# P*V of two key units in one burst, four work banks in one pool, seven P tiles

## The chip, the cores and the metric

The kernel runs on one core of one Trainium2 chip. The metric is the device time of one execution in microseconds (us). The profile is one execution, taken by the hardware profiler; its times count from the first instruction of the span.

## The reference

One layer gates between two branches that read the same x of 2048 rows and 512 columns. All tensors are bf16.

```python
g = sigmoid((x * gate_w).sum(-1, keepdims=True))
out = g * A(x) + (1 - g) * B(x)

# B: gated GELU, inner width 1792
B = (gelu(x @ w_gate) * (x @ w_up)) @ w_down

# A: 32 heads of 16, four segments of 512 rows; causal inside a segment, a memory across segments
for s in range(4):
    p     = softmax(qs @ ks.T / 4 + causal_mask)
    a_dot = p @ vs
    a_mem = (phi(qs) @ M) / (phi(qs) @ z + 1e-6)      # phi(t) = t + 1 if t > 0 else exp(t)
    o     = sigmoid(beta) * a_mem + (1 - sigmoid(beta)) * a_dot
    M += phi(ks).T @ vs;  z += phi(ks).sum(rows)
A = concat(o) @ wo
```

## The kernel before

Everything stays on chip between the loads of x and the weights and the stores of the result. The work is cut into the four segments of 512 rows. Per segment there are projections of Q, K and V, the memory terms, the attention, and the three products of the gated GELU. The last product and the output projection accumulate into the same PSUM bank, in groups of 18 full matmuls (14 of `w_down`, 4 of `wo`). The other full groups have four matmuls of 512 columns, and then ScalarE or VectorE empties the bank (lines 441, 438, 847, 868).

**Attention.** The 32 heads are taken in four units of eight heads (`t`) per segment, 16 units in all. Four heads of a unit share one instruction group: one half `j = 0`, the other half `j = 1`; these halves are the two "key units" (they use `kpad_0` and `kpad_1`). The logits are computed transposed, keys on partitions, by matmuls on four row tiles of 32 (line 737) into the four banks `X` (one tensor, `psXALL`). The causal triangle packs into five fills per unit, in the order A0, B0, C, A1, B1; C holds a block of each half. Each fill is followed by one exp on ScalarE over 128x2048 elements into a P tile (`PT`, line 745), and by one or two masks on GpSimd for the diagonal blocks (line 757). P*V of one half (function `pv`, line 770) is a burst of 16 matmuls on four column tiles, four key blocks by four heads, with 512, 384, 256 and 128 columns. It needs A, B and C of its half. The values carry a column of ones, so that the sum of the softmax comes out as column 17. VectorE then transposes the bank into `Tb` (line 778), and `norm` (lines 781 to 800) divides, scales and adds the result to the memory's part.

**PSUM.** Eight banks: four are `X`, one is `Pb` for P*V alone (`psP`), and three are a pool `psW0` to `psW2` for all other groups. A group (`Grp`) takes a bank of the pool at its first matmul and gives it back after the instruction that empties it.

**P tiles.** Six, taken in turn; P*V of half 0 frees A0 and B0 before A1 and B1 are filled, in the order of the program's text.

**The order of the work.** A planner (`Sched.schedule`) simulates the five engines with estimated durations. It picks, over all engines, the ready task that can start first, and among equals the one with the highest priority: the longest path to the end plus an entry of the table `BIAS` for its name. The result is one fixed order per engine; semaphores then guard what depends on what. Full groups are issued in pieces of two matmuls, so that logits steps can come between. A task of P*V (`tiled == "pv"`) has rules of its own (lines 191 to 195): when it is ready and the last thing on TensorE was a logits step, it goes at once; otherwise its start counts as 3 us later (`PATIENCE`), except for the very last half of a segment.

Of the kernel before, what the change touches and what calls it, by code (L numbers as in the profile page):

```python
# [11 lines left out]
F32 = mybir.dt.float32  # L12
# [8 lines left out]
P = 128  # L21
ATT_SCALE = 0.25
EPS = 1e-6
R_PT = 6
N_W = 3
PSUM_KEYS = ("X", "P", "W")
DMA_RATE = 330.0e3
PATIENCE = 3.0
OPEN_BONUS = 6.0
BIAS = {  # L30
    "D0": 18, "D1": -562, "D2": 14, "D3": -73, "G0": -139, "G1": 25, "G2": -43, "G3": 47, "GdT0": -152,
    "GdT1": 3, "GdT2": -4, "Gev0": 175, "K0": -203, "K1": 238, "K2": -374, "K3": -9, "Q1": 3, "Q2": 76, "U0":
    171, "U1": 59, "U3": 121, "Um1": 326, "Um2": 354, "Um3": 115, "V0": 4, "V2": 186, "Vev0": 4, "Vev1": -6,
    "Vev3": 31, "den1": 56, "den2": -1, "den3": -5, "denp2": -17, "denp3": -33, "exp0": 78, "exp1": 166,
    "exp2": -1, "exp3": -154, "exsT0": 2, "exsT1": 2, "exsT2": 2, "exsT3": -9, "fin0": 4, "fin1": 14, "fin3":
    -350, "gate0": 9, "gate1": -152, "gelu0": 224, "gelu1": 4, "gelu2": 15, "gelu3": -19, "gexs0": -69,
    "gexs1": -410, "gexs2": 50, "gts0": 4, "gts1": 2, "gts2": 84, "gts3": 40, "kp0": -1283, "kp1": -135,
    "kp2": 26, "kp3": -7, "msk1": 189, "msk2": -33, "msk3": 3, "mz0": 100, "mz2": -453, "mzacc0": -243,
    "mzacc1": 341, "mzacc2": -115, "mzbd0": 25, "mzbd1": -47, "mzbd2": 70, "norm0": 47, "norm1": 44, "norm2":
    -15, "norm3": 382, "num1": 15, "num2": 4, "num3": 54, "nump1": -275, "nump2": -19, "nump3": 84, "oTd1":  # L40
    187, "oTd2": -109, "omg": -23, "pkT0": -16, "pkT1": -268, "pkT2": 70, "pkc0": 270, "pkc1": -17, "pkc2":
    -442, "pke0": -30, "pke1": -21, "pke2": 380, "pqc1": -30, "pqc2": -20, "pqc3": -25, "pqe1": 5, "pqe2": -6,
    "pqe3": 79, "pv0": -19, "pv1": 2, "pv2": 64, "pv3": 95, "pvt0": 1, "pvt1": -237, "pvt2": -42, "pvt3": -2,
    "qk0": 224, "x1": 389, "x3": 21
}
HOP = {PE: 0.17, ACT: 0.07, DVE: 0.07, POOL: 0.10, SP: 0.0}

# [66 lines left out]
class Sched:  # L114
# [32 lines left out]
    def schedule(self):  # L147
# [35 lines left out]
        while len(order) < n:  # L183
            best = None
            due = min([ready_at[t.id] for t in ready[ACT] if t.tiled == "exp"] + [1e9])
            for e in ENGINES:
                for t in ready[e]:
                    st = max(cur[e], ready_at[t.id])
                    if e == ACT and t.tiled != "exp" and st + t.est[e] > due + 0.1:
                        continue  # L190
                    if t.tiled == "pv":
                        if last_pe == "qk" and ready_at[t.id] <= cur[e]:
                            best = ((-1.0, 0.0, t.id), e, t)
                            continue
                        st += t.patience
                    if t.grp is not None and t.grp.bank is None:
                        if not bank_free:
                            continue
                        st = max(st, min(bank_free.values()))
                    open_ = t.grp is not None and t.grp.bank is not None  # L200
                    k = (st, -t.prio - (OPEN_BONUS if open_ else 0.0), t.id)
                    if best is None or k < best[0]:
                        best = (k, e, t)
            assert best is not None, "deadlock in task graph"
            (st, _, _), e, t = best
            if t.tiled == "pv":
                st = max(cur[e], ready_at[t.id])
            if e == PE:
                last_pe = t.tiled
            for a in t.alts:  # L210
                ready[a].discard(t)
            t.eng = e
            t.start = st
            t.finish = st + t.est[e]
            cur[e] = t.finish
            avail = t.finish
            if t.nbytes:
                dma_free = max(t.finish + 2.2, dma_free) + t.nbytes / DMA_RATE
                avail = dma_free
            g = t.grp  # L220
            if g is not None:
                if g.bank is None:
                    g.bank = min(bank_free, key=lambda b: bank_free[b])
                    del bank_free[g.bank]
                g.left -= 1
                if g.left == 0:
                    bank_free[g.bank] = t.finish + HOP[e]
            order.append(t)
            for s in t.succs:
                npred[s.id] -= 1  # L230
                hop = 0.0 if (e == PE and s.alts.keys() == {PE}) else HOP[e]
                ready_at[s.id] = max(ready_at[s.id], avail + hop)
                if npred[s.id] == 0:
                    for a in s.alts:
                        ready[a].add(s)
# [103 lines left out]
def dve_t(n, mode=1, psum=False, ap=False):  # L339
    return max(0.19, 0.155 + n / mode / 960.0 + (0.06 if ap else 0.0))  # L340
# [11 lines left out]
def _build(es, nc, A_x, A_wq, A_wk, A_wv, A_wo, A_beta, B_w_gate, B_w_up, B_w_down, gate_w, out):  # L352
    def sb(name, shape, dtype=BF):
        return es.enter_context(nc.sbuf_tensor(name, shape, dtype))
# [9 lines left out]
    Vaug = [sb(f"vaug{i}", [P, 4, 32, 17]) for i in range(2)]  # L364
    otok = sb("otok", [P, 4, 512])
    oT = [sb(f"oT{i}", [P, 4, 512]) for i in range(2)]
    Tb = [sb(f"tb{i}", [P, 2, 512], F32) for i in range(2)]
    obf = [sb(f"obf{i}", [P, 512]) for i in range(2)]
    ott = [sb(f"ott{i}", [P, 512]) for i in range(2)]
    hT = [sb(f"hT{i}", [P, NFT, 512]) for i in range(2)]  # L370
# [30 lines left out]

    XALL = es.enter_context(nc.psum_tensor("psXALL", [P, 2048], F32))
    X = [XALL[:, g * 512:(g + 1) * 512] for g in range(4)]
    Pb = es.enter_context(nc.psum_tensor("psP", [P, 512], F32))
    banks = []
    for i in range(N_W):
        w = es.enter_context(nc.psum_tensor(f"psW{i}", [P, 512], F32))
# [12 lines left out]
    def task(name, eng, instrs, **kw):  # L420
        return S.add(Task(name, {eng: instrs}, **kw))
# [69 lines left out]
    for c0, c1 in ((0, 128), (128, 512)):  # L491
        for key, w, src in (("wk", wk, A_wk), ("wq", wq, A_wq)):
# [9 lines left out]
    wdma("wd", SP, wd[:], r4(B_w_down), 1835008)  # L502
    wdma("wo", SP, wo[:], r4(A_wo), 524288)

    task("warmP", PE, [Instr(lambda e: e.matmul(Pb[:, :], warm[:, 0:128], warm, start=True, stop=True), [wkey],
                             [("P",)], 0.43)], bias=5001.0)
    for i in range(8):
        gw = Grp(banks)
        task(f"warm{i}", PE, [Instr(lambda e, gw=gw: e.matmul(gw.f32()[:, :], warm[:, 0:128], warm, start=True,  # L509
                                                              stop=True), [wkey], [gw.key], 0.43)],  # L510
             grp=gw, bias=5000.0 - i)
# [213 lines left out]
    def attention(s):  # L725
        sl = s % 2
        for t in range(4):
# [32 lines left out]
                task(f"msk{s}_{t}{name}", POOL, minstrs)  # L760
                return slot

            def pv(j, sa, sbk, sc):
                i2 = t % 2
                instrs = []
                for kb in range(4):
                    slot, c0 = ((sa, 0), (sbk, 0), (sc, 256 * j), (sbk, 384))[kb]
                    for q in range(4):
                        h = 8 * t + 2 * q + j
                        instrs.append(Instr(lambda e, q=q, kb=kb, slot=slot, c0=c0, h=h: e.matmul(  # L770
                            Pb[32 * q:32 * q + 17, 128 * kb:512], Vaug[sl][:, kb, h, :],
                            PT[slot][:, q, c0:c0 + 512 - 128 * kb], start=(kb == 0), stop=(kb == 3),
                            tile_position=(0, 32 * q)),
                            [("PT", slot), ("Vaug", sl, kb)], [("P",)], 0.043))
                p = task(f"pv{s}_{t}_{j}", PE, instrs)
                p.tiled = "pv"
                p.patience = 0.0 if (t, j) == (3, 1) else PATIENCE
                task(f"pvt{s}_{t}_{j}", DVE, [Instr(lambda e: e.transpose(Tb[i2][:, j, :], Pb[:, :]),  # L778
                                                    [("P",)], [("Tb", i2, j)], dve_t(512))])

            def norm():
                i2 = t % 2
                tv = Tb[i2][:].rearrange("p j (b c) -> p j b c", c=32)
                ov = bass.AP(obf[i2], 0, [[512, P], [16, 2], [32, 16], [1, 16]])
                rb = sc1[i2][:].rearrange("p j (b o) -> p j b o", o=1).to_broadcast([P, 2, 16, 16])
                gd = GdT[sl][:, 2 * t:2 * t + 2, :]
                ok = [("oT", sl, qt, t) for qt in range(4)]
                dst, dk = (oT[sl][:, t, :], ok) if s == 0 else (ott[i2][:], [("ott", i2)])
                ins = [
                    Instr(lambda e: e.reciprocal(recip[i2][:], tv[:, :, :, 16]), [("Tb", i2, 0), ("Tb", i2, 1)],  # L790
                          [("recip", i2)], 0.35),
                    Instr(lambda e: e.tensor_tensor(sc1[i2][:], recip[i2][:], gd, ALU.mult),
                          [("recip", i2), ("GdT", sl)], [("sc1", i2)], 0.34),
                    Instr(lambda e: e.tensor_tensor(ov, tv[:, :, :, 0:16], rb, ALU.mult),  # L794
                          [("Tb", i2, 0), ("Tb", i2, 1), ("sc1", i2)], [("obf", i2)], 0.79),
                    Instr(lambda e: e.transpose(dst, obf[i2][:]), [("obf", i2)], dk, dve_t(512))]  # L796
                if s > 0:
                    ins.append(Instr(lambda e, t=t: e.tensor_tensor(oT[sl][:, t, :], oT[sl][:, t, :], ott[i2][:],  # L798
# [3 lines left out]
            a0 = fill("A0", [(0, 0, 512, 0)], [0])  # L802
            b0 = fill("B0", [(0, 1, 384, 0), (0, 3, 128, 384)], [0, 384])
            cc = fill("C", [(0, 2, 256, 0), (1, 2, 256, 256)], [(0, 256)])
            pv(0, a0, b0, cc)
            a1 = fill("A1", [(1, 0, 512, 0)], [0])
            b1 = fill("B1", [(1, 1, 384, 0), (1, 3, 128, 384)], [0, 384])
            pv(1, a1, b1, cc)
            norm()

    gelu_of = {}
# [197 lines left out]
```

## Time and profile before

| | us |
|---|---|
| median of three executions | 281.25 |
| lowest and highest | 280.67 and 281.27 |
| the profiled execution | 280.67 |
| its span, first to last instruction | 279.0 |
| TensorE busy | 267.8 (96%) |
| ScalarE busy | 215.4 (77%), of it 150.1 in 80 exps of 1876 ns |
| VectorE busy | 192.1 (69%) |
| GpSimd busy | 103.8 (37%), of it 83.8 in masks |
| P*V bursts on TensorE, line 770 | 23.1, 512 matmuls |
| transposes of P*V, line 778 | 22.8, 32 of 713 ns |

In the profile PE is TensorE's matmuls, PEld its weight loads, ACT is ScalarE, DVE VectorE, POOL GpSimd and SP the queue that issues DMAs. Busy time of a matmul includes a modelled end that overlaps the next one, so a row of n matmuls of 512 columns is longer than n steps. A few matmul records are missing from a trace; the loads then show one more than the matmuls. In the chain of work each piece has its start, its length and its line; a piece begins where the one that released it ended.

### The profile page before, as it was taken

The page shows a single profiled execution, that of the slowest core. Times are in us where ns is not written, and L with a number is a line of the kernel's source. Part 1 is how long each engine was busy: PE and PEld are TensorE (multiplying, and loading weights), DVE is VectorE, ACT ScalarE, POOL GpSimd, SP SyncE. Part 2 cuts the span into 40 slices and gives each one's busy share as a digit, 9 for nine tenths or more (in the row PEclk, how much of TensorE's full clock was granted, in tenths as well). Part 3 has the DMA queues.
Part 4 walks back from the last instruction along what each step waited for, and adds up shares of the span by engine and source line. Part 5 has one row for each costly group of instructions (what it writes and reads, how often), then busy time and mean ns, then how long its engine had stood idle before and what let it go on. Part 6 is the DMA issues. An engine that isn't in the chain of part 4 may idle for free.

```text
span 279.0 us, 5322 instructions
## 1 busy us (share of the span) xinstructions
PE 267.8 (96%) x2148; PEld 113.4 (41%) x2186; DVE 192.1 (69%) x334; ACT 215.4 (77%) x168; POOL 103.8 (37%) x197
## 2 busy tenths in 40 slices
PE   8999999999999999999999999899999999999995
PEld 3443334344444434543443343334344335443342
DVE  1587999979786997899509897667542657584442
ACT  3788988789989967788779887767878676687622
POOL 8156438531004245734102348434400334333410
PEclk9999999999999999999999999999999999999999
DMA  6999930000022331011000300100000000130002
GB/s 194 200 382 359 206 59 2 0 4 0 0 58 57 40 75 59 19 40 38 2 0 19 59 0 2 36 22 2 21 0 0 0 4 2 37 77 22 18 2 75
DMA packets 29697, 15.30 MB, mean 55 GB/s; under 512 B 21224, under 2 KB 29672, under 8 KB 29672
## 3 DMA queue, kind: packets, MB, share of 16 engines
q1 hardware_dynamic: 29672, 14.96, 22.6%
q8 instruction: 17, 0.28, 0.4%
q14 instruction: 8, 0.07, 0.1%
HBM read 8.14 MB, written 2.10 MB: 37 GB/s over the span
## 4 chain that ended last, share of the span: by engine, by line
PE 87%; DVE 5%; ACT 4%; issue 2%; POOL 1%; ACTq 0%; DVEq 0%
PE psW L424 68%; PE psXALL L737 9%; PE psP L770 6%; ACT pt L745 4%; DVE kpad_1 L624 2%; PE psXALL L424 1%; PE psW L509 1%; DVE hT L868 1%; POOL pt L757 1%; DVE hT L441 0%; DVE oT L798 0%; DVE otok L684 0%; DVE obf L794 0%; PE psXALL L514 0%; DVE ott L796 0%
## 5 line engine op out<-in xcount | busy, mean ns | idle before, releaser
L745 ACT ACTIVATE pt<-psXALL 128x2048 bf16<-128x2048 f32 x80 | 150.1, 1876 | 41.1 <-PE psXALL L737 27.1
L757 POOL TENSOR_SCALAR_AFFINE_SELECT pt<-pt 128x512 bf16<-128x512 bf16 (+1 forms) x112 | 83.8, 750 | 159.5 <-ACT pt L745 150.7
L868 DVE TENSOR_TENSOR hT<-psW,hT 128x512 bf16<-128x512 f32 x56 | 37.1, 685 | 26.7 <-PE psW L424 26.5
L424 PE MATMUL psW<-xT,wu 128*128 128x512 bf16 x217 | 51.4, 380 | 1.4 <-issue 0.6
L424 PE MATMUL psW<-xT,wg 128*128 128x512 bf16 x215 | 50.6, 380 | 1.3 <-issue 0.8
L424 PE MATMUL psW<-wd,hT 128*128 128x512 bf16 x201 | 50.1, 380 | 1.0 <-issue 0.8
L778 DVE STREAM_TRANSPOSE tb<-psP 128x512 f32<-128x512 f32 x32 | 22.8, 713 | 22.5 <-PE psP L770 22.4
L424 PEld LDWEIGHTS psW<-xT,wu 128*128 128x128 bf16 x224 | 20.3, 97 | 27.8 <-DVE hT L868 2.9
L424 PEld LDWEIGHTS psW<-xT,wg 128*128 128x128 bf16 x224 | 20.4, 98 | 26.2 <-issue 2.1
L424 PEld LDWEIGHTS psW<-wd,hT 128*128 128x128 bf16 x210 | 18.6, 98 | 22.4 <-issue 4.0
L770 PE MATMUL psP<-pt,vaug 128*17 128x256 bf16 (+3 forms) x512 | 23.1, 300 | 0.0
L847 ACT ACTIVATE hT<-psW 128x512 bf16<-128x512 f32 x28 | 16.3, 597 | 6.1 <-PE psW L424 6.1
L424 PE MATMUL psW<-xT,wk 128*128 128x512 bf16 x60 | 15.9, 379 | 0.7 <-issue 0.3
L737 PE MATMUL psXALL<-qT,kpad_0 32*128 32x512 bf16 (+3 forms) x256 | 15.8, 301 | 0.4 <-ACT exs L641 0.2
L737 PE MATMUL psXALL<-qT,kpad_1 32*128 32x512 bf16 (+3 forms) x256 | 15.8, 301 | 0.3 <-ACT pt L745 0.3
L424 PE MATMUL psW<-xT,wq 128*128 128x512 bf16 x61 | 15.3, 379 | 0.5 <-DVE mzacc L710 0.2
L424 PE MATMUL psW<-wo,oT 128*128 128x512 bf16 x56 | 14.6, 380 | 0.9 <-DVE ost L896 0.7
L424 PE MATMUL psW<-wv,xT 128*128 128x512 bf16 x62 | 15.3, 380 | 0.1
L441 DVE CAST hT<-psW 128x512 bf16<-128x512 f32 x21 | 14.0, 680 | 1.8 <-PE psW L424 1.6
L770 PEld LDWEIGHTS psP<-pt,vaug 128*17 128x17 bf16 x512 | 10.0, 89 | 12.9 <-issue 5.3
L652 POOL COPY exsT<-exs 32x4 f32<-32x4 f32 x64 | 13.5, 212 | 3.6
L836 ACT ACTIVATE hT<-hT 128x2048 bf16<-128x2048 bf16 (+2 forms) x6 | 12.7, 2184 | 0.0
(92 smaller groups left out, 241.0 us busy)
## 6 DMA issues: line engine op xcount, KB each, us to landing
out_dram<-ost SPq DMA_DIRECT2D x16, 128.0 KB, 1.7
wg<-in_B_w_gate_dram SPq DMA_DIRECT2D x2, 896.0 KB, 6.0
wu<-in_B_w_up_dram SPq DMA_DIRECT2D x2, 896.0 KB, 10.5
wd<-in_B_w_down_dram SPq DMA_DIRECT2D x1, 1792.0 KB, 16.6
hT<-in_A_x_dram SPq DMA_DIRECT2D x2, 256.0 KB, 2.9
wv<-in_A_wv_dram SPq DMA_DIRECT2D x1, 512.0 KB, 5.9
wo<-in_A_wo_dram SPq DMA_DIRECT2D x1, 512.0 KB, 12.9
wq<-in_A_wq_dram SPq DMA_DIRECT2D x1, 384.0 KB, 5.0
```

Of the source, the lines that this page charges most:

```text
L424: return Instr(lambda e: e.matmul(view(), lhsT, rhs, start=first, stop=last), reads=reads, writes=[fkey if fkey is not None else g.key], e ...
L441: alts[DVE] = [Instr(lambda e: e.tensor_copy(dst(), src()), reads=reads, writes=writes, est=dve_t(n))]
L624: Instr(lambda e, j=j: e.tensor_scalar(kpad[j][sl][:], kT[:], maskc[j][:, 0:1], None, ALU.mult), [("kT", t) for t in range(4)] + [("c", "m ...
L652: cross = task(f"exsT{s}", POOL, [Instr(lambda e, g=g, c=c: e.tensor_copy(exsT[sl][32 * g:32 * g + 32, c:16:4], exs[32 * c:32 * c + 32, s4 ...
L737: instrs.append(Instr(lambda e, t=t, g=g, j=j, kb=kb, ncol=ncol, c0=c0: e.matmul(X[g][:, c0:c0 + ncol], kpad[j][sl][32 * g:32 * g + 32, t, ...
L745: prev_exp[0] = exp_task(s, f"exp{s}_{t}{name}", [Instr(lambda e: e.activation(PT[slot][:], XALL[:, :].rearrange("p (g c) -> p g c", g=4), ...
L757: minstrs.append(Instr(lambda e, view=view, pat=pat: e.affine_select(out=view, in_=view, compare_op=ALU.is_ge, fill=0.0, base=0, pattern=p ...
L770: instrs.append(Instr(lambda e, q=q, kb=kb, slot=slot, c0=c0, h=h: e.matmul(Pb[32 * q:32 * q + 17, 128 * kb:512], Vaug[sl][:, kb, h, :], P ...
L778: task(f"pvt{s}_{t}_{j}", DVE, [Instr(lambda e: e.transpose(Tb[i2][:, j, :], Pb[:, :]), [("P",)], [("Tb", i2, j)], dve_t(512))])
L836: t = task(f"gelu{s}_{f0}", ACT, [Instr(lambda e, hv=hv: e.activation(hv, hv, ACTF.Gelu_apprx_tanh), hk, hk, act_t(512 * n, False) + (0.0 ...
L847: lambda e, g=g, ft=ft, s=s: e.activation(hT[s % 2][:, ft, :], g.f32()[:, :], ACTF.Gelu_apprx_tanh),
L868: task(f"Um{s}_{ft}", DVE, [Instr(lambda e, g=g, ft=ft: e.tensor_tensor(hT[sl][:, ft, :], g.f32()[:, :], hT[sl][:, ft, :], ALU.mult), [g.k ...
```

## The change

- `Pb` is gone. The pool has four banks in place of three, and each P*V burst takes a bank of the pool as any group does; its transpose gives the bank back.
- Both halves of P*V are placed after the fifth fill, and both wait for the last mask of B1 (`joint`). The planner sends a ready burst at once behind a logits step or behind another burst, if a bank is free at that moment. The second of a pair is planned 0.11 us shorter.
- While bursts are ready, or will be within 0.3 us, the planner keeps that many banks from other groups (`held`).
- There is no patience for any burst of the last unit of a segment.
- Seven P tiles in place of six. One `Tb` in place of two.
- The table `BIAS` has new entries throughout, so the planner's order is another on every engine.
- The warm-up matmul that wrote `Pb` becomes the ninth of those that write the pool.

```diff
-R_PT = 6
-N_W = 3
-PSUM_KEYS = ("X", "P", "W")
+R_PT = 7
+N_W = 4
+PSUM_KEYS = ("X", "W")
+PV_JOIN = 0.11
+HOLD = 0.3
 BIAS = {
...
+            held = sum(t.tiled == "pv" and ready_at[t.id] <= cur[PE] + HOLD for t in ready[PE])
...
                     if t.tiled == "pv":
-                        if last_pe == "qk" and ready_at[t.id] <= cur[e]:
-                            best = ((-1.0, 0.0, t.id), e, t)
+                        if last_pe in ("qk", "pv") and ready_at[t.id] <= cur[e] and bank_free and \
+                                min(bank_free.values()) <= cur[e]:
+                            if best is None or (-1.0, 0.0, t.id) < best[0]:
+                                best = ((-1.0, 0.0, t.id), e, t)
                             continue
                         st += t.patience
                     if t.grp is not None and t.grp.bank is None:
-                        if not bank_free:
+                        if len(bank_free) <= (0 if t.tiled == "pv" else held):
                             continue
...
+            if e == PE:
+                if t.tiled == "pv" and last_pe == "pv":
+                    t.finish -= PV_JOIN
+                last_pe = t.tiled
...
-    Tb = [sb(f"tb{i}", [P, 2, 512], F32) for i in range(2)]
+    Tb = sb("tb", [P, 2, 512], F32)
...
-    Pb = es.enter_context(nc.psum_tensor("psP", [P, 512], F32))
...
-            def pv(j, sa, sbk, sc):
-                i2 = t % 2
+            def pv(j, sa, sbk, sc, joint):
+                gp = Grp(banks)
...
-                            Pb[32 * q:32 * q + 17, 128 * kb:512], Vaug[sl][:, kb, h, :],
+                            gp.f32()[32 * q:32 * q + 17, 128 * kb:512], Vaug[sl][:, kb, h, :],
...
-                p = task(f"pv{s}_{t}_{j}", PE, instrs)
+                p = task(f"pv{s}_{t}_{j}", PE, instrs, grp=gp, after=joint)
                 p.tiled = "pv"
-                p.patience = 0.0 if (t, j) == (3, 1) else PATIENCE
+                p.patience = 0.0 if t == 3 else PATIENCE
...
             cc = fill("C", [(0, 2, 256, 0), (1, 2, 256, 256)], [(0, 256)])
-            pv(0, a0, b0, cc)
             a1 = fill("A1", [(1, 0, 512, 0)], [0])
             b1 = fill("B1", [(1, 1, 384, 0), (1, 3, 128, 384)], [0, 384])
-            pv(1, a1, b1, cc)
+            joint = [S.tasks[-1]]
+            pv(0, a0, b0, cc, joint)
+            pv(1, a1, b1, cc, joint)
             norm()
```

## The prediction

> **What bounds the kernel now.** I read the page first: busy times, the slices, the chain. TensorE is the engine that ends the program. It is busy for 96% of the span at the full granted clock, and the slices show no stage in which it rests. The DMA is quiet after the first sixth.
>
> ```profile
> span 279.0 us, 5322 instructions
> ...
> PE 267.8 (96%) x2148; PEld 113.4 (41%) x2186; DVE 192.1 (69%) x334; ACT 215.4 (77%) x168; POOL 103.8 (37%) x197
> ...
> PE   8999999999999999999999999899999999999995
> ...
> PEclk9999999999999999999999999999999999999999
> ...
> PE 87%; DVE 5%; ACT 4%; issue 2%; POOL 1%; ACTq 0%; DVEq 0%
> ```
>
> The chain is 87% TensorE. So the time moves by what TensorE no longer spends, or by what it newly waits for. Busy is not the same as useful, because the ends of matmuls are modelled. So I read next the chain in order of time, where each piece begins at the moment at which the one before lets go.
>
> ```profile
> 95.21 0.33 PE psXALL L737 x8
> 95.54 0.65 PE psP L770 x16
> 96.19 0.34 PE psW L424 x4
> ...
> 98.26 0.33 PE psXALL L737 x8
> 98.59 2.26 PE psW L424 x10
> ```
>
> A logits step (line 737) takes 0.33 us, whether a P*V burst (line 770) or full matmuls (line 424) follow. The burst then adds 0.65 us before full work goes on. The timeline of one stretch in attention of segment 1 gives the rate of full matmuls:
>
> ```profile
> 101.11 2.33 PE L424 MATMUL psW<-wd,hT 128*128 128x512 bf16 x10
> 103.38 0.40 PE L737 MATMUL psXALL<-qT,kpad_1 32*128 32x384 bf16 x8
> 103.70 0.49 PEld L770 LDWEIGHTS psP<-pt,vaug 128*17 128x17 bf16 x16 [0.21 <-issue]
> 103.71 0.72 PE L770 MATMUL psP<-pt,vaug 128*17 128x512 bf16 x16
> 104.36 1.41 PEld L424 LDWEIGHTS psW<-wd,hT 128*128 128x128 bf16 x8 [0.16 <-issue]
> 104.48 0.72 DVE L778 STREAM_TRANSPOSE tb<-psP 128x512 f32<-128x512 f32 x1 [0.26 <-PE psP L770]
> 104.59 1.67 PE L424 MATMUL psW<-wd,hT 128*128 128x512 bf16 x7 [0.16 <-issue]
> ```
>
> Ten matmuls of 512 columns last 2.33 us and seven last 1.67 us, so one step is 0.66 / 3 = 0.22 us. A burst streams 512 + 384 + 256 + 128 = 1280 columns (its four column tiles side by side), which is 2.5 steps or 0.55 us. It occupies 0.65 us. So 0.10 us of each burst is entering and leaving the column-tiled arrangement. Eight loads but seven matmuls stand after the burst: one matmul record is missing, and the idle 0.16 "issue" before it is no wait.
>
> Last come TensorE's own waits. Without the opening and the rows called issue they are small, about 2.8 us in all:
>
> ```profile
> PE psW L424 <- issue: 2.7, 17, 0.2
> PE psP L505 <- DVE pt L482: 1.3, 1, 1.3
> PE psW L424 <- DVE ost L896: 0.7, 1, 0.7
> PE psW L424 <- DVE hT L868: 0.5, 1, 0.5
> ```
>
> TensorE never waited on psP at line 770: the rows show no such wait. So the separate P bank costs nothing by waiting. What can be gained is the entering and leaving, and a part of 2.8 us.
>
> **The change, part by part.** The profiled execution took 280.67 us, 279.0 of it span and 1.67 around it. The three times shown are 280.67, 281.27 and 281.25, so their median lies 0.58 us above the profiled run. I make the sum as a difference, from the profiled run's rows, and put it on the median.
>
> *Joined bursts.* There are 32 bursts, 16 units of two. The matmuls and columns stay the same. Now both bursts of a unit become ready together, after the last mask of B1, and the planner puts the second right behind the first. No row of before shows a burst after a burst. Upper bound of the gain: the second burst costs its streaming alone, 16 x 0.10 = 1.6 us (1.8 if the step is read as 0.216). Lower bound: nothing is saved, 0, if the pair is not adjacent in the order. A loss would need the join to cost more than the entry and exit that it replaces. The burst itself argues against that: it holds four column blocks with fresh weights each, and all 16 loads end 0.49 us after the start while the matmuls run for 0.72, so weights for the next block are loaded under running matmuls. I take 1.6, since a block that follows a block inside the burst is the nearest row.
>
> The Trainium skill, page "TensorE: Matmul & The Clock Gate", Part 3 on row and column tiling, speaks against the join: a weight load overlaps a running matmul only where the row group differs. All P*V loads use all 128 rows. By that rule the second burst would wait out the first one's last matmul (some 0.22 us) and a load (0.09), and the pairs would lose 16 x (0.31 - 0.10) = 3.4 us. The rows above show loads under running matmuls of the same rows, so I go by the rows.
>
> *The bank pool.* The P bank becomes a fourth work bank. Between bursts all other groups have four banks in place of three; from the moment a pair is ready until it starts, the planner keeps two for it, so others have two; after it, they have two until the first transpose has read its bank, then three, then four. On the gain side TensorE's waits bound it: of the 2.8 us, some 2.3 are for a bank or an operand out of VectorE. On the loss side: a group of four full matmuls lasts 4 x 0.22 = 0.88 us. With two banks its bank must be emptied within the next group. By the timeline, a burst's last matmul to the transpose that reads it is at most 0.1 us after its modelled end, and a full matmul's modelled end lies 0.16 us past its step (0.38 against 0.22). So emptying by line 868 or 441 takes 0.16 + 0.1 + 0.69 = 0.95 us, 0.07 more than the cover, and 0.75 more if one other VectorE operation is ahead. How long are only two left? The mask of B1 ends some 1.4 us after its exp, the next free logits step comes at 2.6 us (the pace of the exps, from 101.37 to 103.96), so for some 1.2 us per pair: one or two group changes. Long groups (18 matmuls of down and output projection, 3.9 us) don't change banks then and cover it. Bounds: -2.3 to 16 x 0.75 = +12; both far. I take 0.07 twice in ten of the pairs, +1.4, against half of the 2.3, -1.1: together +0.3, because VectorE is busy 69% on average and the planner can put long groups there.
>
> *Order of VectorE, and one Tb.* The two transposes (0.72 us each) now stand one behind the other, and the normalization of a unit (lines 790 to 798: 0.35, 0.31, 0.69, 0.71, 0.55) follows as before. With one Tb, the next unit's transposes wait for the third of these; they come one unit, five exps or 13 us, later. Nothing, under that cover. Without the cover it would be 1.4 us once per unit.
>
> *Seven P tiles.* A unit fills five tiles and all five now stay until the pair has run, so two exps of the next unit can go ahead and the third waits for the pair. Counted from the end of the B1 exp, the third starts 5.2 us later; mask 1.4, wait for a logits step to 2.9, the pair 1.2: done at 4.1. Nothing, with 1.1 us to spare. If the pair misses that logits step and takes the next, ScalarE stands for 1.5 us, but ScalarE is 77% busy, so most is absorbed.
>
> *The end.* The last burst ran from 268.64, its transpose from 269.42; the last addition into oT ended at 272.67 and TensorE had other work until then. With a pair, the second transpose waits for the first: 0.4 us later. TensorE's remaining independent work is the same. I take +0.1; ends 0 and +0.4.
>
> *The bias table.* All its entries are new, so every engine's order is new. That is not a cost of instructions but of waits. The bounds come from TensorE's idle share by stage in before:
>
> ```profile
> 82.00:136.00 54.00, 52.27 (x498) 23.12 (x506) 44.96 (x77) 44.94 (x34) 23.92 (x43) 1.00 0.23 46
> 136.00:150.00 14.00, 13.79 (x70) 5.96 (x71) 5.64 (x11) 11.00 (x15) 0.64 (x1) 1.00 0.00 0
> ```
>
> The stages run from 1.5% idle (136 to 150) to 3.2% (82 to 136); from 6 to 270 us the sum is 6.8 us idle, 2.6%. All at the worst stage's share would be +1.7 us, all at the best's -2.8. Nothing says which way, so I take 0 and keep both ends. The ninth warm-up matmul moves from P to the pool: the same count, nothing.
>
> **Sum.** -1.6 + 0.3 + 0.1 = -1.2 us: 279.5 for an execution like the profiled one, 280.0 against the median of 281.25.
>
> **The rivals.** *Reserved banks starve TensorE (slower).* The place is the second before each pair in stages of short groups (gate, up, projections), where only two banks remain. For it: VectorE's slices show it full in much of the first 115 us, so an emptying operation often has one ahead, at 0.75 us a time. Against it: the planner knows its own reservation, and TensorE's waits on banks are small today with three. It decides from 1.5 / 16 = 0.09 us per pair beyond what I took for free; at one queued operation (0.75) in five pairs and 0.1 in the others it is 4.9 us against 1.6 gained plus what the fourth bank gives back: some +1.5 to +2.5, 282.8 to 283.8; mild forms give 281.9.
> *Gain eaten.* The pairs join, but waits of the new order (its end is +1.7) return all: 280.7 to 281.8. For it: TensorE is so full that any displaced wait shows. Against: the new order may as well be the better one.
> *The fourth bank pays too.* Join 1.6 and most of the 2.3 of bank waits: 278.0 to 279.0. For it: bursts hold two banks for only 2 us of each 16; against: the waits are spread over many places, and not all are for banks.
> *The pairs don't join.* The second burst finds no bank and goes behind another logits step: the saving shrinks towards 0 and the time lies within the "gain eaten" band.
>
> **How the numbers follow.** Forecast (279.1 to 280.6): 0.45. Fourth bank pays: 0.12. Gain eaten or not joined: 0.13. Starved: 0.30. A change within 0.2% (0.56 us) is about what a measurement of this kernel cannot tell from none. So faster 0.57, same 0.13, slower 0.30. The range 278.6 to 283.0 leaves out some 0.05 below and 0.12 above; the forecast's own range is 279.1 to 280.6.
>
> **What would show it.** In the chain of the changed kernel a pair should last 0.65 + 0.55 = 1.20 us with 32 matmuls; 16 such rows confirm the join. TensorE's waits on banks (psW after line 868, 441 or 778) should stay near 2.8 us in all; over 4.4 means starved. ScalarE should not wait for line 770. I am wrong if pairs come apart, if the pair lasts above 1.3 us, or if the order brings new TensorE waits of over 1 us.

## The result and the profile after

The changed kernel takes 278.41 us (four executions, 278.16 to 278.99), the kernel before 280.96 in the same comparison (280.66 to 281.27). The ratio is 0.9912, with a 95% interval of 0.9891 to 0.9933: 2.5 us faster, between 1.9 and 3.1. The prediction had 280.0 and a range of 278.6 to 283.0. The direction is right. The gain is twice the forecast one, and the time lies 0.2 us below the range. It falls into the band of a rival, "the fourth bank pays too" (278.0 to 279.0), which had 0.12; what follows shows that this rival is, in the main, also what happened.

The profiled execution took 278.39 us, 276.7 of it span. These are the rows of its page that answer to those shown of before:

```profile
span 276.7 us, 5333 instructions
...
PE 265.9 (96%) x2147; PEld 114.8 (41%) x2186; DVE 196.7 (71%) x336; ACT 213.1 (77%) x166; POOL 101.5 (37%) x197
...
PE   8999999999999999999999999899999999999995
...
PEclk9999999999999999999999999999999999999999
...
PE 81%; ACT 6%; DVE 4%; POOL 2%; issue 2%; DMA 2%; SPq 1%; DVEq 0%; ACTq 0%; POOLq 0%
```

TensorE still ends the program, at the same clock and with the same share of its span. Nothing has become the bound in its place. The chain in order of time shows the pairs:

```profile
38.38 0.33 PE psXALL L741 x8
38.71 1.20 PE psW L774 x32
39.91 0.97 PE psW L430 x4
40.88 0.35 PE psXALL L741 x8
...
95.46 0.33 PE psXALL L741 x8
95.78 1.20 PE psW L774 x32
```

A pair of 32 matmuls takes 1.20 us, where two single bursts took 2 x 0.65. In the timeline all 32 weight loads of a pair end 1.03 us after its first, while its matmuls run for 1.26:

```profile
38.64 1.03 PEld L774 LDWEIGHTS psW<-pt,vaug 128*17 128x17 bf16 x32 [0.21 <-issue]
38.64 1.26 PE L774 MATMUL psW<-pt,vaug 128*17 128x512 bf16 x32
```

In the trace 15 of the 16 units are joined: 13 pairs follow a logits step and two follow full matmuls. The last unit's bursts stay apart, at 265.4 and 267.4, each between full matmuls.

TensorE's own waits are these:

```profile
PE psW L430 <- issue: 2.7, 17, 0.2
PE psW L513 <- DVE pt L488: 1.3, 1, 1.3
PE psW L430 <- DVE hT L873: 1.1, 3, 0.6
PE psXALL L741 <- ACT pt L749: 0.5, 2, 0.3
PE psW L430 <- DMA wq<-in_A_wq_dram: 0.3, 1, 0.3
PE psW L774 <- ACT hT L852: 0.2, 1, 0.2
```

Without issue and the opening that is 2.1 us, against 2.8 before. These rows miss short waits and shorten the long ones, since a matmul's modelled end hides up to 0.16 us after its step. So I also took every step from one matmul's start to the next, less its columns at the full rate (0.216 us for 512), less the usual entry or exit (0.09 to 0.11). Where a weight load stands without its matmul, the missing matmul is counted in: 38 before, 39 after. What remains above 0.025 us is waiting. From the end of the warm-up matmuls on it is 5.0 us at 26 places before and 3.5 us at 13 places after:

| waiting of TensorE, us | before | after |
|---|---|---|
| first 10 us | 0.2 | 0.7 |
| full matmuls into a `psW` bank, from 10 us on | 3.6 at 19 places | 1.8 at 4 places |
| logits steps | 1.2 | 0.7 |
| P*V | 0 | 0.3 |

More than half of the 0.7 in the first 10 us is the late load of wq. The second line is the waiting for banks and operands in steady work. Of the four places that are left, the longest (0.77 us, until 194.9) stands behind VectorE: there the chain runs from a pair at 188.2 through its two transposes and the normalization to the operation that empties the bank:

```profile
188.20 0.68 PE psW L774 x16
188.91 1.31 DVE tb L782 x2
...
194.23 0.61 DVE hT L873
194.89 1.04 PE psW L430 x4
```

The last emptying of a bank starts at 273.54 us where it started at 276.06, so TensorE is done 2.5 us earlier. What follows takes 3.2 us in place of 2.9.

### The profile page after: what moved, and what is told of

It is laid out like the page before. It is cut to its first block, busy times and chain, and to the rows that moved or that the text cites. A ratio compares the mean times of both kernels' runs of the same rounds, so it can differ in the third digit from the quotient of the medians.

```text
span 276.7 us, 5333 instructions
## 1 busy us (share of the span) xinstructions
PE 265.9 (96%) x2147; PEld 114.8 (41%) x2186; DVE 196.7 (71%) x336; ACT 213.1 (77%) x166; POOL 101.5 (37%) x197
## 4 chain that ended last, share of the span: by engine, by line
PE 81%; ACT 6%; DVE 4%; POOL 2%; issue 2%; DMA 2%; SPq 1%; DVEq 0%; ACTq 0%; POOLq 0%
PE psW L430 65%; PE psXALL L741 8%; PE psW L774 6%; ACT pt L749 5%; DMA wq<-in_A_wq_dram 2%; PE psXALL L430 1%; POOL exsT L656 1%; SPq L461 1%; POOL pt L761 1%; DVE hT L873 1%; ACT L852 1%; DVE ost L901 1%; DVE tb L782 0%; ACT hT L852 0%; DVE ndsc L678 0%
## 5 line engine op out<-in xcount | busy, mean ns | idle before, releaser
L761 POOL TENSOR_SCALAR_AFFINE_SELECT pt<-pt 128x512 bf16<-128x512 bf16 (+1 forms) x112 | 81.1, 727 | 156.0 <-ACT pt L749 134.0
L782 DVE STREAM_TRANSPOSE tb<-psW 128x512 f32<-128x512 f32 x32 | 21.1, 697 | 21.6 <-PE psW L774 21.4
L774 PE MATMUL psW<-pt,vaug 128*17 128x256 bf16 (+3 forms) x512 | 20.4, 300 | 0.2 <-ACT hT L852 0.2
L447 DVE CAST hT<-psW 128x512 bf16<-128x512 f32 x20 | 13.1, 680 | 3.4 <-PE psW L430 3.4
L774 PEld LDWEIGHTS psW<-pt,vaug 128*17 128x17 bf16 x512 | 10.7, 90 | 10.5 <-issue 3.5
L901 DVE TENSOR_SCALAR ost<-psW,omgt 128x512 bf16<-128x512 f32 x10 | 7.3, 748 | 9.8 <-PE psW L430 9.8
```

The costliest lines, as they stand in the source:

```text
L447: alts[DVE] = [Instr(lambda e: e.tensor_copy(dst(), src()), reads=reads, writes=writes, est=dve_t(n))]
L761: minstrs.append(Instr(lambda e, view=view, pat=pat: e.affine_select(out=view, in_=view, compare_op=ALU.is_ge, fill=0.0, base=0, pattern=p ...
L901: DVE: [Instr(lambda e, view=view, gt=gt, tile=tile: e.tensor_scalar(ostage[tile][:], view(), omgt[:, gt:gt + 1], None, ALU.mult), rd, [(" ...
```

## The experiments

Two theories had to be told apart. *Join*: the time is saved where a burst no longer enters and leaves the column tiles by itself. *Pool*: TensorE waits less because there are four banks for all groups. Against both stood *order*: the new table alone gives a better order. All ratios are to the kernel before in the same comparison; the changed kernel stands at 0.9912. Where I give a difference to the changed kernel in microseconds, it is the difference of the two ratios times 281; it carries both intervals, together about 0.7 us.

**A burst apart, by full matmuls (e2).** The planned order stays, but the piece of two full matmuls that follows a pair is moved between its bursts, in all 15 pairs. (In this diff and the next two, comment lines in words stand for the inserted code.)

```diff
-    for t in S.schedule():
+    order = list(S.schedule())
+    # for each second burst t at i that follows a first, nxt being the next task of TensorE:
+    #     order[i:nxt + 1] = tasks that don't need t, then t, then those that do
+    for t in order:
         for ins in t.alts[t.eng]:
             em.plan(t.eng, ins)
```

> The changed kernel, but two full matmuls stand between the two bursts of every joined pair (the piece that followed the pair). Theory join: each pair now leaves the column tiles once more and enters them once more without a logits step to share it, 0.099 + 0.096 us as the trace has these steps; 15 x 0.195 = +2.9 us, so 281.3. Rival free: no more than +0.5 us. A rival from the Trainium skill (TensorE: Matmul & The Clock Gate, Part 3: weight loads overlap running matmuls only where the row group differs): the join itself would cost 0.3 us, and parting the bursts would win 15 x 0.1 = 1.5 us, 276.9; the pair's 1.20 us in the chain speaks against it.

Measured: 281.78 us, ratio 1.0026 (1.0010 to 1.0041). That is 3.2 us over the changed kernel, 0.21 us for each pair. The chain of e2 around the pair shown above:

```profile
38.89 0.65 PE psW L774 x15
39.54 0.54 PE psW L430 x2
40.08 0.65 PE psW L774 x16
40.73 0.54 PE psW L430 x2
41.27 0.33 PE psXALL L741 x8
```

From the first burst to the logits step it takes 2.38 us. The changed kernel needs 1.20 + 0.97 = 2.17 for the same work. The 0.21 us is one exit and one entry, and nothing covers it. Waiting, counted as above, is 3.6 us in e2, nearly that of the changed kernel. So entering and leaving cost what theory join says, and TensorE is the bound. The rival by which a join costs 0.3 us for a weight load that has to wait is out: parting the pairs lost time, and the loads of a pair run under its matmuls.

**The second burst behind the next logits step (e1, e5).** This was meant as the arrangement of before in an otherwise fixed order.

```diff
-    for t in S.schedule():
+    order = list(S.schedule())
+    # e1: 12 second bursts move behind the next logits step, with what needs them up to there
+    # e5: 11 of them; what needs them moves behind all tasks planned to start before the burst's new end
```

> The changed kernel with its planned order, but in the 12 units where a logits step follows, the second P*V burst is moved behind the next logits step, as in the kernel before. All other instructions keep their order. Theory join (entering and leaving costs 0.09 to 0.11 us per burst, and TensorE is the bound): 12 x 0.1 = +1.1 to +1.3 us over the changed kernel's 278.4, so 279.5 to 279.7, and the chain shows bursts of 0.65 us in place of pairs of 1.20. Rival free (the join saves nothing that isn't covered; the gain is all in waits): 278.2 to 278.6.

> As e1, but the transpose that reads the moved burst is moved back in VectorE's order too, behind the operations planned to start before the burst's new end; in e1 it stood right behind the first transpose and VectorE waited for TensorE there (43.7 us in all before line 782, against 21.4 in the changed kernel). 11 units are changed. Theory join: 11 x 0.1 = +1.1 us over the changed kernel, 279.5 to 279.9. Rival queue (the price of parting a pair in a fixed order is in the waits behind it, since the bank is held 3 us longer and VectorE's order is only roughly mended): over 281.5. Rival free: 278.2 to 278.7.

Measured: e1 291.06 us, ratio 1.0356 (1.0334 to 1.0377); e5 285.44 us, ratio 1.0167 (1.0150 to 1.0183). Both are far above every theory of the join. In e1 VectorE stood at the second transpose: it waited 43.7 us in all before line 782, against 21.4 in the changed kernel, and everything behind it in its queue waited too. In e5 that is mended in part (34.9 us). What is left shows in TensorE's waits of e5 and in its timeline:

```profile
PE psXALL L741 <- ACT pt L749: 5.8, 13, 0.5
```

```profile
39.40 0.72 PE L774 MATMUL psW<-pt,vaug 128*17 128x512 bf16 x16
40.06 1.04 PE L430 MATMUL psW<-xT,wq 128*128 128x512 bf16 x4
41.59 0.40 PE L741 MATMUL psXALL<-qT,kpad 32*128 32x256 bf16 x8 [0.50 <-ACT pt L749]
```

The second burst had been the work that TensorE did while ScalarE read the logits. Taken away from there, the next logits step comes 0.55 us too soon and waits for the exp: 13 waits, 5.8 us. So the times of these two runs don't price the join. They show what a task is worth as cover in a fixed order: in e5 7.2 us over the changed kernel, 0.65 us for each of 11 units, six times the switching cost. Counted step by step, 1.2 us of e5's loss are entries and exits, 0.11 for each of the 11 bursts as theory join has it, and the rest is waiting. The rival *queue* had the time right (over 281.5), but the waits are those of logits steps for ScalarE more than those for a bank.

**Banks at a fixed order (e3).** The order is that of the changed kernel, instruction for instruction. Only the bank numbers are dealt anew.

```diff
+    # banks in the planned order: P*V takes bank 3, or any free one where bank 3 is taken;
+    # all other groups take one of banks 0 to 2 (19 groups that find none take bank 3)
```

> The changed kernel with its planned order, but the banks are dealt anew: all groups other than P*V take one of three banks, and the fourth is for P*V, except for 19 groups that would find none. Nothing else changes. Theory pool (the waits of TensorE for a work bank that went away, some 1.2 us, went because there is a fourth): most of them come back, +0.8 to +2 us, 279.2 to 280.4, and TensorE waits for psW after VectorE and ScalarE again at many places. Rival order (the waits went because the new order table deals better with what there is): within 0.3 us, 278.1 to 278.7.

Measured: 285.76 us, ratio 1.0175 (1.0148 to 1.0202), 7.4 us over the changed kernel. Theory pool holds in direction, but the price is far beyond the expected 0.8 to 2. TensorE's waits in e3:

```profile
PE psW L430 <- ACT hT L852: 2.7, 2, 1.3
PE psW L430 <- DVE hT L873: 2.4, 4, 1.0
...
PE psW L430 <- DVE tb L782: 0.3, 1, 0.3
```

Waits for a bank are longer: 5.1 us in six waits after lines 852 and 873, where the changed kernel has 1.1 in three, and up to 1.0 and 1.3 us each. By the starts of the matmuls, the waits on `psW` from 10 us on, without that for the load of wq, are 8.4 us at 17 places, against 1.8 at four. Entries and exits are the same in both, so what e3 loses is waiting. The order of the changed kernel leans on four banks that go to whoever comes. Rival order, in the sense that the number of banks would not matter, is out for this order.

**The pool without the join (e4).** Four banks and seven tiles, but each half of P*V goes where it went before, with the patience of before; the table was searched anew for this arrangement.

```diff
...
-                        if last_pe in ("qk", "pv") and ready_at[t.id] <= cur[e] and bank_free and \
+                        if last_pe == "qk" and ready_at[t.id] <= cur[e] and bank_free and \
...
             cc = fill("C", [(0, 2, 256, 0), (1, 2, 256, 256)], [(0, 256)])
+            pv(0, a0, b0, cc, ())
...
-            joint = [S.tasks[-1]]
-            pv(0, a0, b0, cc, joint)
-            pv(1, a1, b1, cc, joint)
+            pv(1, a1, b1, cc, ())
```

> Pool of four banks, seven P tiles, one Tb, but P*V of half 0 is placed after the fill C and goes behind a logits step as in the kernel before; nothing is joined. The order table was searched anew for this arrangement. Theory sum (join 1.3 and pool 1.2 add up): 1.3 over the changed kernel, 279.7, with few waits for psW banks. Rival pool is worth nothing by itself (it only makes room for the join): 281.0, like the kernel before. Rival join worth nothing: 278.4.

Measured: 280.67 us, ratio 0.9984 (0.9970 to 0.9997). By itself the pool gives 0.45 us, between 0.1 and 0.8, and the join on top of it 2.0. (Of the 2.6 us between the two profiled spans, 1.5 are entries and exits, the rest mostly waits.) The expectation of a plain sum (279.7) missed by 0.8 us when both are taken as ratios. TensorE's waits in e4:

```profile
PE psXALL L745 <- ACT pt L753: 1.2, 3, 0.7
PE psW L434 <- DVE hT L876: 0.9, 2, 0.5
PE psW L778 <- POOL pt L765: 0.7, 1, 0.7
PE psW L434 <- DVE vaug L451: 0.3, 1, 0.3
```

Taken from the matmuls' starts as above, the waits on `psW` from 10 us on are 1.7 us at five places: as few as in the changed kernel, and half of before. But other waits are longer than before: 1.0 us in P*V (before none), 1.4 for logits steps (before 1.2) and 0.8 in the first 10 us (before 0.2). The most of P*V's is one place (third row):

```profile
35.40 4.70 POOL L660 COPY exsT<-exs 32x4 f32<-32x4 f32 x16
40.24 1.97 POOL L765 TENSOR_SCALAR_AFFINE_SELECT pt<-pt 128x512 bf16<-128x512 bf16 x3
41.63 0.51 PE L778 MATMUL psW<-pt,vaug 128*17 128x384 bf16 x12 [0.70 <-POOL pt L765]
```

This burst is half 1 of a unit. After its first key block it stands until GpSimd has masked B1, and GpSimd began that only after 16 copies that this order has ahead of it. So the pool takes away bank waits without the join too, and this order gives the gain back elsewhere. Whether another order of e4 would keep more of it stays open: one order per arrangement was run.

**Six tiles (e6).** The changed kernel with `R_PT = 6`, the table searched anew.

```diff
-R_PT = 7
+R_PT = 6
...
```

> The changed kernel with six P tiles, its order table searched anew. A unit fills five tiles that all stay until its pair has run, so one exp of the next unit can go ahead and the second waits for the pair. From the end of the B1 exp the second starts 2.6 us later and the pair ends 4.1 later: 1.5 us in 15 units, 22 us of ScalarE. Theory tiles (the seventh tile is needed for the join): ScalarE is 77% busy and can hide part, TensorE the rest by other work only as far as it has any: 281 to 288, and ScalarE waits for line 774 or TensorE for exps. Rival (hidden): 278.2 to 279.0.

Measured: 282.28 us, ratio 1.0069 (1.0045 to 1.0093), 4.4 us over the changed kernel. ScalarE waits for P*V, as theory tiles has it; the changed kernel has no such row:

```profile
ACT pt L753 <- PE psW L778: 6.0, 7, 1.0
```

Of the 22 us of delay that were expected on ScalarE, its rows show 6.0, and the program is 4.4 us longer. How much of the 4.4 comes from the tile and how much from the new table is not separated. In this order, with six tiles the join costs more than it brings.

**The join without the pool (e7).** Two banks for P*V alone, two for all other groups, seven tiles; the table searched anew. Two of the nine warm-up matmuls write the P*V banks.

```diff
-N_W = 4
+N_W = 2
...
-                        if len(bank_free) <= (0 if t.tiled == "pv" else held):
+                        if not bank_free:
...
+    Pb = [es.enter_context(nc.psum_tensor(f"psP{i}", [P, 512], F32)) for i in range(2)]
...
-                            gp.f32()[32 * q:32 * q + 17, 128 * kb:512], Vaug[sl][:, kb, h, :],
+                            Pb[j][32 * q:32 * q + 17, 128 * kb:512], Vaug[sl][:, kb, h, :],
...
```

> Joined bursts and seven tiles, but two banks belong to P*V alone and two are the pool of all other groups; the order table is searched anew. Theory pool (the join pays only because its banks go back to the pool): a group of four matmuls covers 0.86 us and emptying a bank takes 0.95, so at nearly every one of some 170 changes of short groups TensorE waits 0.1 to 0.8 us: over 290. Rival (two are enough, long groups cover): 278.4 to 280.

Measured: 297.7 us, ratio 1.0606 (1.0588 to 1.0625). TensorE's waits in e7 are on every neighbour, and many are too short for these rows:

```profile
PE psXALL L751 <- ACT pt L759: 5.1, 13, 1.0
PE psW L436 <- DVE hT L882: 2.3, 4, 1.2
PE psP L783 <- POOL pt L771: 2.0, 3, 1.2
PE psW L436 <- DVE otok L698: 1.2, 3, 0.6
```

The starts of the matmuls give 20.7 us of waiting between tasks and 2.5 us inside bursts, against 3.5 in all in the changed kernel: that is the whole of the 19.5 us by which e7 is longer. 12.6 us of it are waits on `psW` at 61 places. Joined bursts need two banks, and these can't be taken from the others for good. Pool and join belong together: the pool alone gives 0.45 us (e4), the join without the pool loses 17 us against the kernel before.

*Order* is not tested by itself: no run has the kernel before with another table. Two things speak against it as the whole cause. e2 changes the order at the pairs alone and loses what entries and exits cost. And the waits on `psW` are 1.8 and 1.7 us in two different orders with four banks (the changed kernel and e4), against 3.6 with three and 12.6 with two (e7). But four banks alone do not make such waits rare: e6 has four, and 5.1 us of them (not counting eight steps at half the granted clock). So how much of the saved waiting is the pool's and how much the table's stays open.

## Why the prediction was half right

- *The bound.* TensorE's own time decides: right. e2 adds 0.21 us to each of 15 pairs and the program is 3.2 us longer.
- *Joined bursts, -1.6.* The price of 0.10 us per burst is right: a pair takes the 1.20 us foretold. The sum is a little smaller, since 15 pairs are joined where I had 16. Before, 30 bursts stood behind a logits step (0.10 each) and two between full matmuls (0.20 each, as e2 shows): 3.4 us. After, 13 pairs behind a logits step, two pairs and the two parted bursts between full matmuls: 1.3 + 0.8 = 2.1. Saved: 1.3.
- *The Trainium skill's rule against the join* ("TensorE: Matmul & The Clock Gate", Part 3: loads overlap running matmuls only where the row group differs) does not hold for these column tiles: the pair's loads run under its matmuls, and the join costs nothing.
- *The bank pool, +0.3: this is the step that failed.* It had a starving of +1.4 in ten pairs and -1.1 for the fourth bank. Measured from the starts of the matmuls, waits on `psW` in steady work fell by 1.8 us, from 3.6 to 1.8. The starving isn't there in the form that I priced: one pair of 15 waited for a bank itself (line 774, 0.3 us, at 200.4), and in the second before a pair there is one wait for a bank, of 0.2 us until 133.5. Both are for an emptying on ScalarE that comes late, behind a load of its function table of 1.28 us (at 198.34 and 131.56). I had priced the reservation by the shortest cover, a group of four matmuls, and taken it that TensorE meets two group changes in that second. I read the result as the planner, which knows the reservation, letting TensorE work in open groups meanwhile; no run tests that reading. The gain was sized too small at its base: I took 2.3 us from the rows of waits, each of which has lost up to 0.16 us to a modelled end. By the steps the base is 3.6, and half of it is what fell away. The new table changed together with the bank, so this term and the next can't be told apart by the result alone; e4 has the same fall under another table.
- *The bias table, 0 with ends -2.8 and +1.7.* All waiting together fell by 1.1 us net, which is within these ends (1.5 in the places above 0.025 us; the smaller ones grew by 0.4). I could not have told its sign from before's trace, but I had no reason to put the range's lower end at 278.6 when the ends of pool and table together reached below 278.
- *Seven tiles, nothing; one Tb, nothing.* Right as far as the trace shows: ScalarE's waits of over 0.15 us in the changed kernel include none for line 774. No run has the changed kernel with two `Tb`. That the seventh tile is no luxury is what e6 speaks for: without it ScalarE waits for P*V.
- *The end, +0.1.* What follows TensorE's last work is 0.2 to 0.3 us longer. Right in sign.
- *The sum.* -1.4 of entries and exits (by all steps; 1.3 by the count above), -1.1 of waits and +0.2 at the end is -2.3, the whole of what lies between the two profiled executions (280.67 and 278.39). Between the medians it is 2.5.

## What to carry to other kernels

When one engine is full, take its waits from the starts of its instructions: rows of waits that begin at modelled ends showed 2.8 us where the steps show 5.0. Then count its changes of arrangement and price one by the chain's pieces; that price holds to a few hundredths of a microsecond when the arrangement is changed. A private buffer that one kind of work holds for a fraction of the time is worth more in a common pool, but a burst that needs two at once makes sense only there, and only with enough input buffers behind it. An experiment that moves one task in a fixed order measures the loss of its cover before it measures the task: put something of the same length in its place, or leave the distances as they are.

## What I had not expected of the hardware

Two column-tiled bursts join without any seam: the second burst's first matmuls start 0.05 us after the last matmuls of the first, the time of their 128 columns, although they use new weights and another bank. Also, a bank less for the other groups at a fixed order costs 7.4 us (e3), where TensorE's own waits before the change were 5.0 us in all: how much a buffer is worth is not seen in the waits of an order that was made for it.
